# Token tiles split by ScalarE and GpSimd and transposed by DMA, an earlier key split, and four score blocks ahead of the products of differences

## The chip, the cores and the metric

The kernel runs on one core of one Trainium2 chip. A core has five engines that run their own instruction queues and meet at semaphores: TensorE (PE, matrix products into PSUM), VectorE (DVE), ScalarE (ACT), GpSimd (POOL) and SyncE (SP, which here only starts DMAs). The profile gives PE's weight loads a row of their own, PEld. The metric is the device time of one execution in microseconds; lower is better.

## The reference

The input is x, 2048 tokens of 512 numbers. With xn the layer norm of x without gain or bias, the result is the sum of three terms:

```
x + Re( DFT_seq( DFT_hid( xn ) ) ) + PEER( xn )
```

The second term is `y = Cr@(xn@Wr.T) - Ci@(xn@Wi.T)`, with cosine and sine matrices along the 2048 tokens and along the 512 numbers. The third is a mixture of 4096 tiny experts: 32 heads make a query of 2 x 128 numbers each, each half is scored against 64 keys (`s1 = q1 . k1`, `s2 = q2 . k2`), the best two of each half give four pairs, the best two pairs by their sum are weighted by a softmax, and the head adds `g * gelu(xn . u[e]) * v[e]` for both experts e.

## The kernel before

There are two long stages after a short opening, and the change lies in the opening.

**Opening (0 to about 71 us).** The tokens are held as four groups g of four 128-token tiles, in a host order in which tokens that are mirror images under the DFT stand in the same partition. The groups are taken in the order `G = (1, 0, 2, 3)`. For each group `ln` makes the layer norm in place (statistics on DVE and ACT, the scaling on ACT), and `fold(k, g)` adds (k = 0) or subtracts (k = 1) mirror tokens and mirror columns on DVE, which leaves a quarter of the products to do. `main(k, g)` on PE then multiplies the folded tokens `Q[k][g]` with the matrix part `A[k, g]` in float32 and accumulates over the four groups in four PSUM banks `PP[k]`; `evict(k)` copies them out with ACT. So the sums (k = 0) take 16 such products, and the products of differences (k = 1) 16 more. They use the same four banks (pool tag `pa`), so the second set waits for `evict(0)`. `sides` makes the rows and columns that the folding leaves over, on DVE and at its end with two instructions of GpSimd (lines 440 and 441). `fold_row` and `spread` do the same for one single row on GpSimd.

Beside that the first key matrix is made. The 32 heads are worked on in 8 chunks j of four. For a chunk, query weights and keys are multiplied once (`m_mul`) to a 512x512 matrix, so that a score block is one product of tokens with it. The matrix is scaled by a power of two (`m_scale`: largest magnitude by ACT, reduced over partitions by GpSimd on line 118, then small DVE steps) and split in a high and a low half-precision part (`m_parts`: lines 219 and 220). `k16` is the split key for the later chunks.

The tokens need the same split, and transposed. `xpose(i)` does it for tile i with four PE transposes into a PSUM bank (line 475) and an ACT copy that makes the high part (line 478). The low part comes, for the eight tiles of the first two groups, from a PE product with a negative identity and another ACT copy (lines 480 and 482), and for the eight of the last two from DVE (line 484). The result `xt[i]` takes the place of the raw tile.

**Scores (about 64 to 430 us).** `scores(j, i)` for 8 chunks times 16 tiles: 12 products (four column blocks times high-high, high-low and low-high) of 128x512 into one `pa` bank, ACT copies to `ss` (line 784), DVE finds the best eight of each group of 64 (line 787) and their places (line 791). Between the blocks the next chunk's key is made: loads of its weights (`m_load`, line 134), their split (`m_prep`, lines 158 to 166, for tile parts 0 and 2 on GpSimd), the products (line 144). The memory of these buffers overlays that of the opening (pool `da`), so they can be filled only once `sides` is done. Each finished token tile is also stored to DRAM (line 845).

**Experts (430 us to the end).** Products with all of u and v, gated by a matrix made from the chosen places.

**Order.** A framework (Tile) puts the instructions of each engine in one fixed order before the run. It goes through them by program order, passes over those that by its own estimates aren't ready, and takes the next one that is. On the chip every engine and every queue then runs its list strictly in that order. SP has eight semaphores for its DMAs, so each DMA there waits for the one eight before it.

The lines below are the functions that the change touches.

Of the kernel before, what the change touches and what calls it, by code (L numbers as in the profile page):

```python
# [8 lines left out]
F32 = mybir.dt.float32  # L9
# [26 lines left out]
def tile_fnet_peer(ctx, tc, x, ca, cb, c5, wt, wf, wr, wq, kt, ut, vn, out):  # L36
# [94 lines left out]
    def m_load(j, pool, ts):  # L131
        for t in ts:
            MS[j, t] = pool(f"wq{j}_{t}")
            nc.sync.dma_start(MS[j, t], wq[j, t // 2, t % 2])
# [105 lines left out]

    MP[0] = stS.enter_context(tc.tile_pool(name="mp0", bufs=1, side="left"))
# [40 lines left out]
    FT = {}  # L282

    def ln(g, n):
# [34 lines left out]
        nc.vector.scalar_tensor_tensor(sm[:, 2], sm[:, 0], -0.5, sm[:, 1], op0=ALU.mult, op1=ALU.mult)  # L319
        nc.vector.scalar_tensor_tensor(rstd[:, g], sm[:, 2], 1.5, sm[:, 1], op0=ALU.add, op1=ALU.mult)  # L320
# [64 lines left out]
    def spread():  # L385

        for a in range(2):
            nc.gpsimd.tensor_scalar(s5p[:, a].rearrange("o t p -> o (t p)"), s5[:, 0:256], c52[:, a:a + 1], None, op0=ALU.mult)
# [61 lines left out]
    def turn(dst, src, b=None):  # L450
# [3 lines left out]
        if b is None:  # L454
            nc.scalar.activation(d, v, AF.Copy)
            return
        for a in range(2):
            nc.scalar.activation(d[..., a::2], v[..., a::2], AF.Identity, bias=b[:, a:a + 1])
# [7 lines left out]
    idn = cst.tile([P, P], F16, name="idn")  # L466
    nc.gpsimd.tensor_scalar(idn, ident, -1.0 / XS, None, op0=ALU.mult)

    def xpose(i, sub=False):

        p = (pb if sub and i % 2 else pc)(f"xp{i}")
        src = xn(i // 4, i % 4)
        for kd in range(KD):
            c = slice(kd * P, (kd + 1) * P)
            nc.tensor.matmul(p[:, c], src[:, c], ident, start=kd == 0, stop=kd == KD - 1 and not sub,  # L475
                             is_transpose=True, skip_group_check=True)
        pv = p.rearrange("p (k n) -> p k n", k=KD)
        nc.scalar.activation(xt[i][:, 0], pv, AF.Copy, scale=XS)
        if sub:
            nc.tensor.matmul(p, idn, xt[i][:, 0].rearrange("p k n -> p (k n)"), start=False, stop=True,  # L480
                             skip_group_check=True)
            nc.scalar.activation(xt[i][:, 1], pv, AF.Copy, scale=XS)
            return
# [949 lines left out]
```

## Time and profile before

| | us |
|---|---|
| median of 3 runs (lowest, highest) | 1161.41 (1159.83, 1162.46) |
| time of the profiled execution | 1159.45 |
| its span, first to last instruction | 1157.7 |
| PE busy in the span | 1136.5 |
| DVE busy | 934.5 |
| ACT busy | 610.6 |
| GpSimd busy | 245.0 |
| PE from 0 to 34.37 | 20.39 busy |
| PE from 34.37 to 63.60 | 28.85 busy |
| PE from 63.60 to 71.11 | 7.51 busy |

The profiled execution took 1.75 us more than its span, and 1.96 us less than the median of the runs. Times in rows are counted from the span's start. A row of the timeline gives the start, the duration, the engine, the line of the kernel, the operation, what it writes and reads, how many were merged into the row, and in brackets how long the engine had been idle before and what ended that. `PE p L403` are the float32 products of `main`; each of the 32 products shows as two records. `xp` is the bank of a transposed tile, `s` a score block, `m` the key matrix, `ft`, `ff`, `fo` and `q` are the steps of a fold, `pw` the key's power of two, `zt` the transposed routing codes of the third stage. A queue row such as `SPq` is the time in which the queue was held by starting a DMA, not the transfer.

### The profile page before, as it was taken

To read this page: it belongs to the slowest core of one execution; us is meant where nothing else is said; L and a number is where in the kernel's file an instruction comes from. 1 tells how busy PE (TensorE), PEld (TensorE's weight loads), DVE (VectorE), ACT (ScalarE), POOL (GpSimd) and SP (SyncE) were. 2 spreads that over 40 slices of the span, in tenths; PEclk is the share of its full clock that TensorE was granted. 3 is DMA by queue.
4 is the path that set the end of the run, shared out by engine and by line. 5 is a ranking of instruction groups with operands and counts; after the bars stand their busy time and mean duration, and the time that the engine had idled before them with its cause. 6 is when DMAs were issued, how large, how long until landed. Compare 5 with 4: busy or idle time off the path is not lost.

```text
span 1157.7 us, 25371 instructions
## 1 busy us (share of the span) xinstructions
PE 1136.5 (98%) x9930; PEld 724.9 (63%) x9930; DVE 934.5 (81%) x2840; ACT 610.6 (53%) x1056; POOL 245.0 (21%) x232
## 2 busy tenths in 40 slices
PE   6899999999999999999999999999999999999997
PEld 4355555445445459778478479569569559658763
DVE  7987989798898999974994895897886786788670
ACT  5575687687776635354435435535535435433440
POOL 5232464865865410000000000010010000000000
PEclk9999999999999999999999999999999999999999
DMA  9182344243241204261743743644554555451423
GB/s 364 49 294 64 124 139 169 70 164 119 83 159 52 82 11 126 87 213 37 237 157 104 229 166 107 223 159 137 186 163 169 168 174 168 155 174 56 137 75 104
DMA packets 81504, 163.64 MB, mean 141 GB/s; under 512 B 16084, under 2 KB 31323, under 8 KB 81374
## 3 DMA queue, kind: packets, MB, share of 16 engines
q1 hardware_dynamic: 81008, 161.84, 42.2%
q8 instruction: 80, 1.31, 0.5%
q14 instruction: 50, 0.41, 0.1%
q10 hardware_dynamic: 302, 0.08, 0.0%
q0 software_dynamic: 64, 0.00, 0.0%
HBM read 142.69 MB, written 17.63 MB: 138 GB/s over the span
## 4 chain that ended last, share of the span: by engine, by line
PE 93%; DVE 3%; DMA 2%; ACT 1%; issue 0%; POOL 0%; SPq 0%; ACTq 0%; POOLq 0%; DVEq 0%
PE s L779 29%; PE z L908 28%; PE v L991 27%; PE g L946 4%; PE p L403 2%; PE m L144 2%; DVE L L936 1%; PE xp L475 0%; DMA xb<-in_x_dram 0%; DMA x<-in_x_dram 0%; DMA cx<-in_wt_dram 0%; DMA fit<-v_d 0%; DVE act L962 0%; DMA y<-y_d 0%; DVE w L954 0%
## 5 line engine op out<-in xcount | busy, mean ns | idle before, releaser
L908 PE MATMUL z<-xb,u 128*128 128x256 f16 (+1 forms) x3840 | 342.9, 251 | 0.2
L991 PE MATMUL v<-v,act 128*128 128x512 f16 x1536 | 338.6, 379 | 0.0
L908 PEld LDWEIGHTS <-u 128*128 128x128 f16 x3840 | 309.8, 98 | 26.8 <-issue 0.5
L779 PE MATMUL s<-m,xq 128*128 128x512 f16 x1344 | 297.3, 379 | 0.0
L991 PEld LDWEIGHTS <-act 128*128 128x128 f16 x1536 | 147.4, 98 | 171.0
L779 PEld LDWEIGHTS <-xq 128*128 128x128 f16 x1344 | 129.6, 98 | 150.3 <-issue 0.2
L936 DVE TENSOR_TENSOR L<-io_lam,cmp 128x2048 f16<-128x2048 f16 x128 | 155.9, 1218 | 59.1 <-PE g L946 58.9
L915 ACT ACTIVATE act<-z,scl 128x256 f32<-128x256 f32 (+1 forms) x224 | 100.6, 498 | 171.5 <-PE z L908 171.4
L787 DVE MAX8 vals<-ss 128x8 f32<-128x64 f32 x1024 | 152.6, 216 | 12.6 <-ACT ss L784 12.3
L1004 POOL TENSOR_TENSOR y<-y,xr 128x512 f32<-128x512 f32 x15 | 25.2, 1679 | 611.9 <-DMA y<-y_d 455.8
L961 ACT ACTIVATE act<-w 128x1024 f16<-128x1024 f32 x52 | 69.9, 1360 | 92.8 <-DVE w L954 92.1
L791 DVE FIND_INDEX8 idx<-vals,ss 128x8 uint16<-128x256 f32 x256 | 107.2, 419 | 0.0
L954 DVE SCALAR_TENSOR_TENSOR w<-act,scl,g 128x1024 f32<-128x1024 f32 x64 | 80.9, 1274 | 29.7 <-ACT act L915 29.7
L1067 ACT ACTIVATE cx<-cx 128x896 f32<-128x896 f32 x64 | 60.5, 945 | 72.3 <-DVE cx L1047 53.7
L784 ACT ACTIVATE ss<-s,wsc 128x512 f32<-128x512 f32 x112 | 74.7, 680 | 44.3 <-PE s L779 36.6
L962 DVE TENSOR_TENSOR act<-w,act 128x1024 f16<-128x1024 f32 x64 | 84.9, 1328 | 4.2 <-ACT act L961 4.2
L1041 DVE TENSOR_TENSOR cx<-cx 128x512 f32<-128x512 f32 (+2 forms) x84 | 48.4, 610 | 28.0 <-DMA cx<-in_cb_dram 25.0
L946 PEld LDWEIGHTS <-L 128*128 128x128 f16 x2048 | 60.6, 96 | 11.2 <-DVE R L944 1.2
L946 PE MATMUL g<-R,L 128*128 128x32 f16 x2048 | 61.7, 176 | 0.2 <-DVE R L944 0.2
L944 DVE TENSOR_TENSOR R<-R,cmp 128x512 f16<-128x512 f16 x128 | 59.2, 463 | 1.5
L166 POOL TENSOR_TENSOR wq<-wq,wh 128x1024 f16<-128x1024 f32 x26 | 55.4, 2133 | 12.1 <-DVE xq L484 7.9
L941 DVE TENSOR_TENSOR R<-io_c,cmp 128x512 f16<-128x512 f16 x128 | 54.5, 426 | 0.0
(290 smaller groups left out, 1094.3 us busy)
## 6 DMA issues: line engine op xcount, KB each, us to landing
v<-v_d SPq DMA_DIRECT2D x67, 512.0 KB, 4.2
cx<-in_cb_dram SPq DMA_DIRECT2D x64, 448.0 KB, 4.7
wq<-in_wq_dram SPq DMA_DIRECT2D x32, 512.0 KB, 6.0
fit<-in_wq_dram SPq DMA_DIRECT2D x28, 512.0 KB, 5.3
uv<-in_vn_dram SPq DMA_DIRECT2D x16, 512.0 KB, 3.8
uv<-in_ut_dram SPq DMA_DIRECT2D x16, 512.0 KB, 6.4
c<-in_ca_dram SPq DMA_DIRECT2D x8, 512.0 KB, 10.7
y<-y_d SPq DMA_DIRECT2D x16, 256.0 KB, 2.7
```

Of the source, the lines that this page charges most:

```text
L779: nc.tensor.matmul(ps, xt[i][:, l, kd, :], m[:, r, kd, :], start=(n == 0), stop=(n == 3 * KD - 1))
L784: nc.scalar.activation(s.rearrange("p g e -> p (g e)"), ps, AF.Copy, scale=inv)
L787: nc.vector.max(vals[:, i, w, :, h], s[:, g, :])
L791: nc.vector.max_index(idx[:, i, w].rearrange("p k h -> p (k h)"), vals[:, i, w, 0:2].rearrange("p k h -> p (k h)"), s[:, w * HC:g + 1, :]. ...
L908: nc.tensor.matmul(ps if n == 1 else ps.rearrange("p (b n) -> p b n", b=2), ug[:, l, c % 2, kd, :], xb2[:, k0, r, kd, :] if n == 1 else xb ...
L915: nc.scalar.activation(ACT[bb][:, cg * m:cg * m + m, :], pv[:, i], AF.Gelu_apprx_tanh, scale=zsc)
L936: nc.vector.tensor_tensor(L.rearrange("p t (l two) -> p t l two", two=2), io_lam.rearrange("p (l two) -> p l two", two=2).unsqueeze(1).to_ ...
L946: nc.tensor.matmul(p[:, hf, t * NC:(t + 1) * NC], L[:, t, :], R[:, t, :], start=True, stop=True)
L954: nc.vector.scalar_tensor_tensor(w, act[:, :, ts], fw, p.rearrange("p h (n c) -> p c (h n)", c=NC), op0=ALU.mult, op1=ALU.mult)
L961: nc.scalar.activation(w16[..., 0], w, AF.Copy)
L962: nc.vector.tensor_tensor(w16[..., 1], w, w16[..., 0], op=ALU.subtract)
L991: nc.tensor.matmul(pv, w16[:, c, :, l], v_sb[g][:, r, cc, :], start=(n + cc == 0 and k == 0), stop=(n == 15 and cc == 1 and k == 2))
```

## The change

- `xpose` goes, with its identity. In its place `stage(i)` lets ACT write the half-precision high part of the normalised tile and GpSimd subtract it from the tile for the low part, both in token order, into the space of the not yet loaded expert matrix `u`. One DMA transpose from SP then writes the whole `xt[i]`, both parts.
- The layer norm itself scales by 512, which the split did before; everything made from the tokens by `main` is scaled back in the copies out of PSUM (an added scale factor in instructions that were there) and, for the single row, in `spread`.
- The first group's four tiles are staged right after its sums fold. Its raw tiles get buffers of their own, since the differences are still to be made from them. The loads of the third and fourth group's difference matrices and of `wf`, `w2` and one row now stand in SP's program after these four transposes.
- `m_scale`, `m_parts` and `k16` move up from after all sums to after the third group's.
- The score blocks (chunk 0) of the first group's tiles, `s_mm`, are written in the program ahead of the products of differences, into the two `pb` and two `pc` banks. The other groups' tiles are staged in the loop of the differences, the score blocks follow the order of the groups in chunk 0.
- `zs` holds two zeros that are computed from late values, so that the `stage` copies of the first group wait for the second group's layer norm and the others for the key's scale.
- The weights of chunk 1 are loaded from GpSimd's DMA queue instead of SP's.

```diff
     def m_load(j, pool, ts):
         for t in ts:
             MS[j, t] = pool(f"wq{j}_{t}")
-            nc.sync.dma_start(MS[j, t], wq[j, t // 2, t % 2])
+            (nc.gpsimd if j == 1 else nc.sync).dma_start(MS[j, t], wq[j, t // 2, t % 2])
...
+    def s_mm(ps, m, i):
+        n = 0
+        for kd in range(KD):
+            for l, r in ((0, 0), (0, 1), (1, 0)):
+                nc.tensor.matmul(ps, xt[i][:, l, kd, :], m[:, r, kd, :], start=(n == 0),
+                                 stop=(n == 3 * KD - 1))
+                n += 1
+
+    EARLY = {}
...
+    for h in (2, 3):
+        xp[h] = da.tile([P, 2, 512], F32, name=f"x{h}")
...
+    TO = [4 * g + q for g in G for q in range(4)]
...
+    zs = da.tile([P, 2], F32, name="zs")
...
-        nc.vector.scalar_tensor_tensor(sm[:, 2], sm[:, 0], -0.5, sm[:, 1], op0=ALU.mult, op1=ALU.mult)
-        nc.vector.scalar_tensor_tensor(rstd[:, g], sm[:, 2], 1.5, sm[:, 1], op0=ALU.add, op1=ALU.mult)
+        nc.vector.scalar_tensor_tensor(sm[:, 2], sm[:, 0], -0.5 * XS, sm[:, 1], op0=ALU.mult, op1=ALU.mult)
+        nc.vector.scalar_tensor_tensor(rstd[:, g], sm[:, 2], 1.5 * XS, sm[:, 1], op0=ALU.add, op1=ALU.mult)
...
-            nc.scalar.activation(d, v, AF.Copy)
+            nc.scalar.activation(d, v, AF.Copy, scale=1.0 / XS)
...
-    def xpose(i, sub=False):
-
-        p = (pb if sub and i % 2 else pc)(f"xp{i}")
+    def stage(i):
+
         src = xn(i // 4, i % 4)
-        for kd in range(KD):
-            c = slice(kd * P, (kd + 1) * P)
-            nc.tensor.matmul(p[:, c], src[:, c], ident, start=kd == 0, stop=kd == KD - 1 and not sub,
-                             is_transpose=True, skip_group_check=True)
-        pv = p.rearrange("p (k n) -> p k n", k=KD)
-        nc.scalar.activation(xt[i][:, 0], pv, AF.Copy, scale=XS)
-        if sub:
-            nc.tensor.matmul(p, idn, xt[i][:, 0].rearrange("p k n -> p (k n)"), start=False, stop=True,
-                             skip_group_check=True)
-            nc.scalar.activation(xt[i][:, 1], pv, AF.Copy, scale=XS)
-            return
-        nc.vector.scalar_tensor_tensor(xt[i][:, 1], pv, XS, xt[i][:, 0], op0=ALU.mult, op1=ALU.subtract)
+        n = TO.index(i)
+        t = u_sb[3 + n % 10 // 2][:, n % 2].rearrange("p a k n -> p a (k n)")
+        nc.scalar.activation(t[:, 0], src, AF.Identity, bias=zs[:, int(n > 3):int(n > 3) + 1])
+        nc.gpsimd.tensor_tensor(t[:, 1], src, t[:, 0], op=ALU.subtract)
+        nc.sync.dma_start_transpose(xt[i].rearrange("p a k n -> p (a k) n"), t.rearrange("p a d -> p (a d)"))
...
-    for g in G:
+    for g in G[:2]:
         load(1, g)
     wfs = uf[14][:, 0:512]
-    nc.sync.dma_start(wfs, wf)
-    nc.sync.dma_start(w2, wr[:, 0:2].to_broadcast([P, 2]))
-    row512(1, A[1, 0][0:1, 512:1024])
...
         fold(0, g)
+        if n == 1:
+            nc.scalar.activation(zs[:, 0:1], rstd[:, g, 0:1], AF.Copy, scale=0.0)
+            for q in range(4):
+                stage(4 * G[0] + q)
+            for h in G[2:]:
+                load(1, h)
+            nc.sync.dma_start(wfs, wf)
+            nc.sync.dma_start(w2, wr[:, 0:2].to_broadcast([P, 2]))
+            row512(1, A[1, 0][0:1, 512:1024])
...
+        if n == 2:
+            m_scale(0, MS[0, "p"], FF[0, g][:, 0, 0:1])
+            m_parts(0, MS[0, "p"])
+            nc.scalar.activation(zs[:, 1:2], wsc[:, 0:1], AF.Copy, scale=0.0)
+            nc.scalar.activation(k16[:, 0], k_sb, AF.Copy, scale=sk)
+            nc.vector.scalar_tensor_tensor(k16[:, 1], k_sb, sk, k16[:, 0], op0=ALU.mult, op1=ALU.subtract)
     evict(0)
-    m_scale(0, MS[0, "p"], FF[0, G[-1]][:, 0, 0:1])
-    m_parts(0, MS[0, "p"])
-    nc.scalar.activation(k16[:, 0], k_sb, AF.Copy, scale=sk)
-    nc.vector.scalar_tensor_tensor(k16[:, 1], k_sb, sk, k16[:, 0], op0=ALU.mult, op1=ALU.subtract)
+    for i in TO[0:4]:
+        EARLY[0, i] = (pb if i % 2 else pc)(f"s0_{i}")
+        s_mm(EARLY[0, i], M[0][0], i)
     for n, g in enumerate(G):
         fold(1, g)
...
         main(1, g)
         if n:
             for q in range(4):
-                xpose(4 * G[n - 1] + q, n < 3)
+                stage(4 * g + q)
     sides()
     evict(1)
-    for q in range(4):
-        xpose(4 * G[-1] + q)
...
-        def scores(j, i, vals, idx):
+        def scores(j, n, vals, idx):
             m, inv = M[j]
...
+            i = n if j or safe else TO[n]
+            ps = EARLY.pop((j, i), None)
+            if ps is None:
+                ps = pa(f"s{j}_{i}")
+                s_mm(ps, m, i)
```

More of the change, by code (lines that the diff above doesn't have):

```diff
@@ L568, in sums @@
             nc.tensor.matmul(b8[:, 2 * n:2 * n + 2], a256[:, g // 2, c:c + P], w2, start=True, stop=True)
-        nc.scalar.activation(p256, b8[:, 0:16].rearrange("p (n a) -> p n a", n=8), AF.Copy)
+        nc.scalar.activation(p256, b8[:, 0:16].rearrange("p (n a) -> p n a", n=8), AF.Copy, scale=1.0 / XS)
         b5 = pc("b5")
@@ L771, in compact @@
             CMP[b] = cmp
-        def scores(j, i, vals, idx):
+        def scores(j, n, vals, idx):
             m, inv = M[j]
-            ps = pa(f"s{j}_{i}")
-            n = 0
-            for kd in range(KD):
-                for l, r in ((0, 0), (0, 1), (1, 0)):
-                    nc.tensor.matmul(ps, xt[i][:, l, kd, :], m[:, r, kd, :], start=(n == 0),
-                                     stop=(n == 3 * KD - 1))
-                    n += 1
+            i = n if j or safe else TO[n]
[3 more added lines that the diff above has]
+                s_mm(ps, m, i)
             st = sp.tile([P, 520], F32, tag="s", name=f"ss{j}_{i}", bufs=3 if safe else 4)
```

13 lines of the change are left out of this document (6 added, 7 removed).

## The prediction

> **What bounds the kernel now.** I read the page's totals first, then the chain that ended last.
>
> ```profile
> span 1157.7 us, 25371 instructions
> PE 1136.5 (98%) x9930; PEld 724.9 (63%) x9930; DVE 934.5 (81%) x2840; ACT 610.6 (53%) x1056; POOL 245.0 (21%) x232
> PE 93%; DVE 3%; DMA 2%; ACT 1%; issue 0%; POOL 0%; SPq 0%; ACTq 0%; POOLq 0%; DVEq 0%
> ```
>
> PE is busy for 98% of the span and holds 93% of the chain. What leaves PE's list, or lets it go on sooner, moves all that follows; elsewhere only a new wait of PE counts. The change lies in the opening, so next comes the chain there, cut to the stretch from the third group's sums to the last PE transpose, with two pieces further on, and PE's clock by stretches.
>
> ```profile
> by line: PE p L403 62.6%; PE xp L475 15.5%; PE s L779 9.4%; PE xp L480 5.6%; ACT xq L482 3.2%; ACT xq L478 1.4%; ACT xb L478 1.4%; issue 1.0%
> ...
> 62.05 1.72 PE p L403 x4
> ...
> 80.61 0.70 PE m L144 x24
> 81.31 2.59 PE s L779 x12
> ```
>
> ```profile
> 35.21:38.62 3.41, 3.41 (x5) 1.35 (x4) 3.34 (x6) 0.21 (x1) 0.99 (x2) 0.50 0.06 1
> 30.21:34.37 4.16, 0.00 (x1) 0.00 (x0) 3.74 (x10) 2.43 (x5) 4.02 (x7) 1.00 0.35 130
> ```
>
> The first line covers 34.37 to 71.11, 36.74 us. The reader is to see that token transposing holds PE's path for 15.5 + 5.6 + 3.2 + 1.4 + 1.4 = 27.1%, 10.0 us. A record of `main` takes 1.72 / 4 = 0.43 us, a score block 2.59, a quarter of a key matrix 0.70. After 4.16 us without work PE was granted half its clock for 3.41 us, which costs 1.7.
>
> For comparison I need one point that both kernels pass: four score blocks and all of `main` done. By 71.11 PE had 9.4% of 36.74 = 3.5 us of score work behind it; four blocks are 10.4, so the kernel before reaches the point at 71.11 + 6.9 = 78.0.
>
> **The change, part by part.** PE loses the 10.0 us; the four early blocks and `main` only change places. PE's floor is then the end of the sums plus 10.4 us of blocks plus 32 x 0.43 = 13.8 us of differences. What makes it later are the key, the tiles and the next key. Their rows:
>
> ```profile
> 32.13 2.93 ACT L333 ACTIVATE xq<-xq,negm,rstd 128x512 f32<-128x512 f32 x4 [1.73 <-DVE negm L321]
> 41.46 0.68 ACT L196 ACTIVATE m<-m,fo 128x512 f16<-128x512 f32 x1
> 47.97 0.18 ACT L201 ACTIVATION_READ_ACCUMULATOR m<-k_sb 128x1 f32 x1
> ```
>
> ```profile
> 21.72 1.23 DVE L351 TENSOR_TENSOR fo<-ft 128x2 f32<-128x2 f32 x1
> 34.23 0.42 DVE L373 TENSOR_TENSOR q<-fo 128x257 f32<-128x257 f32 x1
> 36.95 0.15 DVE L351 TENSOR_TENSOR fo<-ft 128x2 f32<-128x2 f32 x1
> 38.95 0.42 DVE L372 TENSOR_TENSOR q<-fo 128x257 f32<-128x257 f32 x1
> 49.47 0.17 DVE L119 TENSOR_SCALAR pw<-pw 128x3 f32<-128x3 f32 x1 [0.29 <-POOL pw L118]
> 51.45 2.72 DVE L220 SCALAR_TENSOR_TENSOR m<-m,msc,m 128x512 f16<-128x512 f32 x4
> 61.45 2.46 DVE L410 SCALAR_TENSOR_TENSOR u<-q,c5s,u 128x257 f32<-128x257 f32 x6
> ```
>
> ```profile
> 11.09 0.24 POOL L77 IOTA iof<- 128x128 f32 x1 [10.16 <-issue]
> 21.68 1.25 POOL L378 TENSOR_TENSOR r<-x 1x512 f32<-1x512 f32 x1
> 35.33 0.87 POOL L390 DMA_DIRECT2D s5c<-s_d  x1
> 48.29 1.15 POOL L118 PARTITION_ALL_REDUCE pw<-mx  x1 [12.09 <-ACT m L201]
> 60.37 4.67 POOL L440 TENSOR_TENSOR u<-u,r 1x512 f32<-1x512 f32 x1 [10.93 <-DVE u L431]
> 65.01 0.72 POOL L441 TENSOR_TENSOR u<-u,r 1x257 f32<-1x257 f32 x1
> 73.67 2.13 POOL L166 TENSOR_TENSOR wq<-wq,wh 128x1024 f16<-128x1024 f32 x1 [7.94 <-DVE xq L484]
> ```
>
> ```profile
> L77 POOLq MODIFY_POOL_CONFIG  x2: 11/11/11, 0.9 to 1.0; - x2
> ...
> L118 POOLq MODIFY_POOL_CONFIG  x4: 4/20/37, 36.5 to 81.1; - x4
> ...
> L440 POOLq MODIFY_POOL_CONFIG  x2: 82/82/83, 49.4 to 49.4; - x2
> ```
>
> *Subtractions of the first group.* The nearest row is L166, the same types at double width: 2.13 / 2 = 1.07 us. Four are 4.3, in GpSimd's list between 21.6 and 26, where DVE's norms and folds are what PE waits for. GpSimd and DVE get in each other's way there: the two-column add L351 took 1.23 us while L378 ran and 0.15 later. So the sums end later by 0 (GpSimd was busy with other such adds before) to 4.3 us (DVE stands through all four). I take 1.2, nearer the low end. The last sums fold was ready at 39.4 and then took 8 records, 3.4 us: 42.8, now 44.0.
>
> *Floor.* 44.0 + 10.4 + 13.8 = 68.2.
>
> *The key.* It may start after the third fold (34.65) and ACT's last norm (35.06). ACT's part took from 41.46 to 48.15 with evictions in between, 6.7 us, so it is done by 41.8 at the latest. Then GpSimd reduces. But L118 is preceded by a pair of MODIFY_POOL_CONFIG, by its name a switch of GpSimd's code library; it went off at 36.5, when GpSimd had done its earlier work. Another such pair is needed before ordinary work goes on, and one stands at the kernel's start, ahead of the 10.16 us before L77 that waited on nothing the profile shows. Around L118 both lay in GpSimd's waits of 12.09 and 10.93 us. Now GpSimd is free only after its old work (36.2) plus 4.3, plus 1.0 that I allow for being held up by DVE: 41.5. With 0 to 10.2 us of switch, and 1.15 of reduction, it ends between 43.0 and 52.8. From its end (49.44) to the first low part (51.45 + 0.68) it was 2.7: the key serves PE from 45.7 to 55.5. I take the far end, since 10.16 is the one switch that lies open. By then PE can have done the differences of two groups, 16 records or 6.9 us (44.0 to 50.9), or of three (54.3), as the planner has it. PE waits 0 to 4.6, and 1.7 more for the half clock if it waits the full length; I take 2.5. The point moves to 70.7.
>
> On the switch the Trainium skill (GPSIMD Engine Reference, section Instruction dispatch) says that the first call to a freshly loaded kernel pays about 6 us. The trace's open case is 10.16 us, and I go by it; by the page, the key would come some 4 us sooner, the 2.5 us wait would go, and the sum below would be 2.5 us better.
>
> *The other tiles.*
>
> ```profile
> L768 SPq DMA_TRANSPOSE zt<-z x2: 1183/1248/1312, 431.8 to 433.8; - x2
> ```
>
> ```profile
> c<-in_ca_dram SPq DMA_DIRECT2D x8, 512.0 KB, 10.7
> zt<-z_d SPq DMA_TRANSPOSE x14, 3.7
> ```
>
> A transpose of three 128x128 blocks held SP's queue for 1.2 us and landed 3.7 after its issue. The new ones have eight blocks. Held time: 1.2 if it goes by the DMA, 8/3 of it, 3.3, if it goes by size; I take 2.1, and 2.5 more until it has landed. GpSimd may subtract once its library is back, up to 10.2 us after 52.8: 63.0, first subtraction 64.1, first tile 68.7. PE asks for it at 70.7, so 2.0 us of cover are left. If DVE keeps GpSimd out to the end of `sides` (63.9 before, 65.1 now), the first tile comes at 70.8. At 3.3 a transpose plus a store in between, twelve tiles run slower than the blocks and cost up to 5. I take 1.0: the point is at 71.7.
>
> The four transposes of the first group hold SP for 4 x 1.2 to 3.3 from about 23 on, and the last two difference matrices queue behind them. Issued by 36 and with the median landing of 10.7, they are there at 47, and PE asks for them after 50.9: nothing.
>
> *The next key.*
>
> ```profile
> 65.76 1.76 SPq L134 DMA_DIRECT2D wq<-in_wq_dram  x4
> ```
>
> ```profile
> 70.38 1.15 ACT L158 ACTIVATE wh<-wq,ss 128x1024 f16<-128x1024 f32 x1
> ```
>
> Its four loads went out when L441 had ended (65.73), and its weights were split on GpSimd by 73.67 + 2.13 = 75.8, 10.1 us later; PE took them at 80.61. Now L440 and L441 can come after twelve more subtractions, 63.0 + 12.8 = 75.8, plus 2 to 5.4 of their own, and the loads follow them in GpSimd's queue: ready 10.1 later, at 88 to 91. PE gets to the old place of the first quarter, behind the fifth block, at 74.3. It has other blocks to do if the planner's list puts them first (two banks of four-deep buffers, 20 us). So 0 to 17 us; I take 1.5, near the low end, because the planner passes over what isn't ready.
>
> *At no cost.* ACT:
>
> ```profile
> L478 ACT ACTIVATE xq<-xp 128x512 f16<-128x512 f32 x14 | 7.9, 597 | 1.9 <-PE xp L475 1.8
> L297 ACT ACTIVATE q<-xb 128x512 bf16<-128x512 f32 x2 | 1.3, 632 | 1.2 <-DMA xb<-in_x_dram 1.2
> L484 DVE SCALAR_TENSOR_TENSOR xq<-xp,xq 128x512 f16<-128x512 f32 x8 | 5.2, 686 | 2.5 <-ACT xq L478 2.5
> ```
>
> 16 copies of about 0.63 replace 24 of about 0.6, 10 against 14 us; DVE loses 5.2. The scale by 512 adds no instruction. Scores of the early blocks can be copied out only when `sides` has left its memory, which PE's eight banks cover for 20 us.
>
> **Sum.** The point was at 78.0 and is at 71.7; less 1.5 for the next key the gain is 4.8 us. The profiled execution's 1159.45 becomes 1154.7; against the median, which lies 1.96 higher, 1161.41 - 4.8 = 1156.6.
>
> **Rivals.**
> (a) *GpSimd becomes the bound (slower).* L440, one row of 512, took 4.67 us from 60.37 while DVE's sums of `sides` ran without a gap to 63.9. If each of the twelve subtractions costs that, the last tile is ready at 63.0 + 56 + 4.6 = 123.6. PE wants it at 70.7 + 11 x 2.59 + 4 x 0.70 = 102.0. It waits 21.6, and the gain without tile wait (5.8) turns to a loss of 15.8: 1177.2. It decides from 3.4 us a subtraction (63.0 + 12 x 3.4 + 4.6 = 108.4, 6 late). Against it: L166 took 1.07 per 512 among score instructions, which follow `sides`. If only the first six are slow, the sixth comes at 95.6 where PE wants it at 70.7 + 5 x 2.59 + 3 x 0.70 = 85.8, and the time is 1165.4.
> (b) *The next key is late (slower).* If the planner keeps the old place, PE stands from 74.3 to 88: 13.7 us, 1161.41 - 6.3 + 13.7 = 1168.8. It decides from 6.3 us. For it: the loads moved behind busy GpSimd; against: the list is made anew.
> (c) *The waits eat the gain (no change).* Key wait 4.6 + 1.7 and tile wait 2 instead of 2.5 and 1.0 take the gain to 0: 1161.4.
> (d) *No waits.* Switch as fast as needed, tiles in time: 78.0 - 68.2 = 9.8, with no delay of the sums 11: 1151.
> (e) *Transposes go block by block.* If a transpose of eight takes 8/3 x 3.7 = 9.9 us and the next waits for it, the last of twelve lands at 64.1 + 119 = 183 where PE wants 102: 81 us late, about 1237. Against it: the second of the two from SBUF was started 2.0 us after the first. The Trainium skill (VectorE: DVE Perf Modes, The three transpose paths) has 390 ns on TensorE against 1309 ns by DMA for one 128x128 and advises TensorE where PSUM will do; eight blocks at that price are an estimated 10.5 us, the same case. The held time of 1.2 us for three blocks speaks against it.
>
> **How the numbers follow.** Forecast (gain 2.3 to 8): 0.43. (d), gain over 8: 0.15. (c): 0.14. (a): 0.12. (b): 0.12. (e): 0.04. A measurement of this kernel tells about 0.2%, 2.3 us, from no change. Faster 0.43 + 0.15 = 0.58, same 0.14, slower 0.28. The likeliest case alone runs from 1153.4 to 1159.1. The range goes from (d) less its last tenth, 1150.5, to (b), 1169, which leaves out (e) and the worse half of (a).
>
> **What the changed profile would show.** No `xp` rows on PE, sixteen transposes on SP with a held time of about 2.1 us, GpSimd subtractions of 1.07 us in the open and longer beside DVE. The point (four blocks and 32 products done) at about 72. L118 at 50 to 53 with an idle time put to issue, then a gap before the next GpSimd row of up to 10 us. I am wrong if PE stands over 6 us in one place before 100 us, if the subtractions take over 3.4 us, or if the first key quarter comes later than 90 with PE idle before it.

## The result, and the profile after

The changed kernel is slower. Its median is 1174.09 us over 4 runs (1171.8 to 1175.55) against 1161.62 over 4 runs of the kernel before beside them: ratio 1.0108, 95% interval 1.0086 to 1.0129. The forecast was 1156.6 with a range of 1150.5 to 1169, so sign and range both missed; the slowdown of 1.1% is small, but clear of the noise. The profiled execution took 1175.55, its span is 1173.8 (before 1159.45 and 1157.7): 16.1 us more.

Where these 16.1 us arise shows in one long window. Its columns are the stretch, its length, busy time and instructions of PE, PE's weight loads, DVE, ACT and GpSimd, then PE's granted clock, DMA share and GB/s. Before, then after:

```profile
0.00:133.00 133.00, 118.64 (x644) 67.00 (x645) 111.49 (x420) 84.33 (x177) 52.37 (x63) 0.99 0.49 175
```

```profile
0.00:133.00 133.00, 101.25 (x478) 54.46 (x479) 111.62 (x355) 69.87 (x151) 68.89 (x65) 0.90 0.63 200
```

PE stood idle for 133 - 118.64 = 14.4 us before and 31.7 after, 17.3 more. In half-microsecond windows, busy time times (1 - clock) adds up to 1.7 us lost to a lower clock before and 9.4 after, 7.7 more. That is 25.0 us lost. After 133 us PE has no long gap in either kernel (8.2 us of idle time in all after the change, 6.9 before), which makes it 26.3. The span grew by 16.1, so the work that PE was relieved of is worth about 10 us; its transposes held 7.8 of that (21.1% of 36.74) on the chain before. The change delivered its saving and lost about two and a half times as much, some 70% of it in waits and the rest in a lower clock.

The third group's sums on PE before the change:

```profile
34.37 15.90 PE L403 MATMUL p<-c,q 128*128 128x512 f32 x32 [4.16 <-DVE q L372]
```

PE's timeline after the change, up to the first product of the next key:

```profile
26.44 5.40 PE L419 MATMUL p<-c,q 128*128 128x512 f32 x8 [1.21 <-DVE q L387]
39.53 5.87 PE L419 MATMUL p<-c,q 128*128 128x512 f32 x8 [7.69 <-DVE q L387]
47.13 3.70 PE L419 MATMUL p<-c,q 128*128 128x512 f32 x8 [1.74 <-DVE q L387]
50.67 10.52 PE L245 MATMUL s<-m,xq 128*128 128x512 f16 x48
61.03 13.90 PE L419 MATMUL p<-c,q 128*128 128x512 f32 x32
74.76 4.91 PE L245 MATMUL s<-m,xb 128*128 128x512 f16 x22
91.02 0.59 PE L144 MATMUL m<-sums,wh 128*128 128x64 f16 x8 [11.35 <-ACT ss L639]
```

Here line 419 is `main` (403 before), 245 a score block, 144 a product of the next key. PE waits 7.69 us for the third group's fold, whose products start at 39.53 (34.37 before). The sums end at 50.8. Then four blocks and 32 products run without a gap to 74.8, the point that the kernel before reaches at 78.0: there the change is still 3.2 us ahead. After 22 more score products PE stands for 11.35 us, because the next key's weights aren't there.

Why they aren't is read on GpSimd, ACT and DVE. GpSimd (488 is the subtraction, 456 and 457 the end of `sides`, 134 the loads):

```profile
44.95 0.39 POOL L118 PARTITION_ALL_REDUCE pw<-mx  x1 [5.76 <-DVE fo L373]
53.03 6.00 POOL L488 TENSOR_TENSOR u<-xb,u 128x512 f16<-128x512 f32 x2 [7.69 <-ACT u L471]
59.00 18.24 POOL L488 TENSOR_TENSOR u<-xq,u 128x512 f16<-128x512 f32 x10
77.99 1.43 POOL L456 TENSOR_TENSOR u<-u,r 1x512 f32<-1x512 f32 x1 [0.76 <-DVE u L447]
82.30 0.90 POOL L457 TENSOR_TENSOR u<-u,r 1x257 f32<-1x257 f32 x1 [2.87 <-DVE u L426]
83.49 2.33 POOL L134 DMA_DIRECT2D wq<-in_wq_dram  x4 [0.30 <-POOL u L457]
```

```profile
83.23 1.26 ACT L795 ACTIVATE ss<-s,msc 128x512 f32<-128x512 f32 x2 [7.67 <-POOL u L457]
89.77 1.15 ACT L158 ACTIVATE wh<-wq,ss 128x1024 f16<-128x1024 f32 x1 [2.96 <-DMA wq<-in_wq_dram]
```

DVE, in the third and the last fold of the sums and in `sides`:

```profile
27.25 2.43 DVE L384 TENSOR_TENSOR ft<-xq,xq 128x1024 f32<-128x1024 f32 x1
32.03 3.04 DVE L333 SCALAR_TENSOR_TENSOR ff<-mvs,ff 128x4 f32<-128x4 f32 x1
42.91 0.16 DVE L203 TENSOR_REDUCE mx<-mx 128x1 f32<-128x4 f32 x1 [0.98 <-ACT m L196]
44.04 0.43 DVE L372 TENSOR_TENSOR fo<-ff 128x256 f32<-128x256 f32 x1 [0.98 <-ACT ff L371]
45.37 0.17 DVE L119 TENSOR_SCALAR pw<-pw 128x3 f32<-128x3 f32 x1 [0.57 <-POOL pw L118]
67.30 2.66 DVE L424 TENSOR_SCALAR u<-c,ft 128x512 f32<-128x512 f32 x2
69.89 6.33 DVE L426 SCALAR_TENSOR_TENSOR u<-c,q,u 128x512 f32<-128x512 f32 x4
76.14 3.57 DVE L447 SCALAR_TENSOR_TENSOR u<-c,q,u 128x256 f32<-128x256 f32 x4
```

`sides` ended at 83.20 (65.73 before) and only then gave up its memory: the copies of the scores (795) and the loads (134) start within 0.3 us of it. The first load was used at 89.77. A subtraction took 1.82 us in the row of ten and 3.0 in the row of two. The twelve took 24.2 us, 2.0 each, not the 3.4 each at which rival (a) begins, though two single ones were longer than that (shortest, median and longest in ns):

```profile
L488 POOL TENSOR_TENSOR u<-xb,u x2: 2496/3016/3536, 53.0 to 55.5; 128x512 f16<-128x512 f32 x2
L488 POOL TENSOR_TENSOR u<-xq,u x10: 1329/1599/4143, 59.0 to 75.6; 128x512 f16<-128x512 f32 x10
```

DVE's instructions grew beside them. Line 426 took 1.58 us each, 447 0.89; an instruction on four numbers per partition (333) took 3.04 (0.47 before). DVE ended its part of `sides` at 82.6, 5.4 us after the last subtraction, so it is DVE's delay that dates the end of `sides`.

### The profile page after: what moved, and what is told of

Same layout as the page of the kernel before. It is cut to its first block, busy times and chain, and to the rows that moved or that the text cites. A ratio compares the mean times of both kernels' runs of the same rounds, so it can differ in the third digit from the quotient of the medians.

```text
span 1173.8 us, 25268 instructions
## 1 busy us (share of the span) xinstructions
PE 1133.8 (97%) x9858; PEld 719.8 (61%) x9858; DVE 948.0 (81%) x2832; ACT 607.9 (52%) x1050; POOL 272.6 (23%) x251
## 4 chain that ended last, share of the span: by engine, by line
PE 84%; DVE 9%; DMA 3%; issue 1%; ACT 1%; POOL 1%; SPq 0%; DVEq 0%; ACTq 0%; POOLq 0%
PE s L245 27%; PE z L919 26%; PE v L1002 25%; PE g L957 4%; PE m L144 2%; DVE L L947 1%; DMA cx<-in_cb_dram 1%; DVE ft L384 1%; DVE act L973 1%; DMA wq<-in_wq_dram 1%; DVE w L965 1%; DVE fo L366 0%; DMA x<-in_x_dram 0%; DVE ff L363 0%; DVE R L952 0%
## 5 line engine op out<-in xcount | busy, mean ns | idle before, releaser
L245 PE MATMUL s<-m,xq 128*128 128x512 f16 x1344 | 301.6, 383 | 0.0
L947 DVE TENSOR_TENSOR L<-io_lam,cmp 128x2048 f16<-128x2048 f16 x128 | 158.4, 1237 | 59.1 <-PE g L957 59.1
```

The source lines that it names most:

```text
L245: nc.tensor.matmul(ps, xt[i][:, l, kd, :], m[:, r, kd, :], start=(n == 0), stop=(n == 3 * KD - 1))
L947: nc.vector.tensor_tensor(L.rearrange("p t (l two) -> p t l two", two=2), io_lam.rearrange("p (l two) -> p l two", two=2).unsqueeze(1).to_ ...
```

## The experiments

Theory at the outset: GpSimd's subtractions and DVE's instructions with two inputs hold each other up, the sums and `sides` end late, and the loads that need the memory of `sides` come late. The rivals: the loads were moved to the wrong queue; PE's list has the next key too early; the memory is held by something else in any case; the key's steps, now in the middle of a fold, delay the sums. The diffs are against the changed kernel; where a run is described as another one with something added, it holds that one's edits too. The kernel before had medians of 1161.49 to 1161.95 beside them. Most times came out slower than the theories expected (`mul_late` by 6.6 us, `tail_apart` by 5.7, `tail_first` by 5.6 beyond their ranges), `key_mid` faster by 1.6; `both` and `last_none` alone lie inside. So it is mainly the traces that carry the argument.

**Is it the subtractions?** `lo_copy` leaves the low part of the tokens out: ACT writes the high part twice.

```diff
-        nc.scalar.activation(t[:, 0], src, AF.Identity, bias=...)
-        nc.gpsimd.tensor_tensor(t[:, 1], src, t[:, 0], op=ALU.subtract)
+        nc.scalar.activation(t, src.unsqueeze(1).to_broadcast([P, 2, D]), AF.Identity, bias=...)
```

> ACT writes both halves of a staged tile in one copy of 128x1024, and the subtraction on GpSimd is gone: the low part of the tokens is wrong here. Theory 1 (GpSimd's subtractions and DVE's two-input instructions hold each other up, in the sums and in sides, and with sides the memory of the next weights comes free late): the third group's sums start at 34 to 35 instead of 39.5, sides ends at 65 to 69 instead of 83.2, PE's stand of 11.35 us before the next key's first quarter is under 2 us, and the time is 1174.1 - 5 - 11 - 3 (half clock) = 1155. Rival (the weights are late because they were moved to GpSimd's DMA queue and land beside the token stores, whatever the subtractions do): sums as in theory 1, but the stand stays above 6 us and the time is 1165 to 1168.

Its 2381.5 us (ratio 2.0513, 2.0466 to 2.056) say nothing of the change: without low parts the kernel goes into a second pass (`safe` in the kernel), in which PE is busy for 1136 us once more. Only the opening is read. The third sums start at 35.87 (39.53), `sides` ends at 69.3 (83.2). But the loads still start only at 74.16:

```profile
68.55 0.72 POOL L457 TENSOR_TENSOR u<-u,r 1x257 f32<-1x257 f32 x1
74.16 2.32 POOL L134 DMA_DIRECT2D wq<-in_wq_dram  x4 [4.90 <-ACT u L471]
```

The second cause stands in the brackets: line 471 copies out the products of differences, whose operands share the memory. With four blocks put ahead of them, the products end at 73.5 and the copies at about 74. PE still waits 3.5 us for the key.

`sub_dve` lets DVE subtract all sixteen tiles, `sub_dve12` only the last twelve.

```diff
-        nc.gpsimd.tensor_tensor(t[:, 1], src, t[:, 0], op=ALU.subtract)
+        nc.vector.tensor_tensor(t[:, 1], src, t[:, 0], op=ALU.subtract)
```

> The sixteen subtractions on DVE instead of GpSimd. Theory 1: each costs DVE about 0.7 us, four ahead of the third group's sums (2.8) and twelve ahead of the end of sides (8.4), but nothing is held up any more; third group's sums at 36 to 37.5, sides ends at 73 to 76, the stand of PE shrinks to 1 to 4 us, time 1160 to 1164. Rival (it is DVE's amount of work, not the contention): no better than the changed kernel, 1172 to 1178.

> Only the twelve later subtractions on DVE; the first group's four stay on GpSimd beside the sums' folds. This parts the contention in the sums from that in sides. Theory 1a (the delay of the sums by the first four costs its full 3 to 5 us): 1170 to 1172. Theory 1b (it is hidden, because the last sums fold waits for the key's steps anyway and PE then runs at half clock): early blocks at 50.7 to 51.2 as in both kernels, time 1166 to 1168.

`sub_dve`: 1166.91 us, ratio 1.0042 (1.0028 to 1.0055), 7.2 less than the change. `sub_dve12`: 1169.32, 1.0067 (1.005 to 1.0083). So the last twelve cost 4.8 us and the first four 2.4. DVE in `sub_dve12`, the same stretch:

```profile
69.03 0.67 DVE L488 TENSOR_TENSOR u<-xq,u 128x512 f16<-128x512 f32 x1
69.81 0.88 DVE L424 TENSOR_SCALAR u<-c,ft 128x512 f32<-128x512 f32 x2
70.61 2.73 DVE L426 SCALAR_TENSOR_TENSOR u<-c,q,u 128x512 f32<-128x512 f32 x4
73.26 1.66 DVE L447 SCALAR_TENSOR_TENSOR u<-c,q,u 128x256 f32<-128x256 f32 x4
75.37 2.46 DVE L426 SCALAR_TENSOR_TENSOR u<-q,c5s,u 128x257 f32<-128x257 f32 x6
```

The openings are alike up to the early blocks (50.76 and 50.67), DVE's rows show no idle time from there to the end of `sides` in either, and DVE's part of `sides` ends at 77.8, against 82.6 after the change (80.16 + 2.46 there), though DVE makes twelve more instructions of 0.67, 8.0 us. Twelve subtractions thus cost DVE 8 us when it makes them and 12.8 when GpSimd does. The Trainium skill (SBUF — State Buffer, Who interferes with whom) says that a DVE instruction with two inputs in SBUF contends with a GpSimd instruction that reads SBUF; these rows agree, and show both sides paying: 1.58 instead of 0.68 us for one of line 426, 2.0 on average for a subtraction, of which the quickest took 1.14. Line 424, which reads one tile, was stretched too: 1.33 instead of 0.44.

The first four act in a roundabout way. Without them the third sums start at 36.07 instead of 39.49, but the early blocks start at 50.7 all the same; what remains is that DVE's list, and with it `sides`, ends 2.3 us earlier (GpSimd's last addition starts at 76.58, not 78.92).

**The queue, and PE's list.** `load_sp` puts the loads back on SP; `mul_late` has the program ask for the key's parts four blocks later.

```diff
-            (nc.gpsimd if j == 1 else nc.sync).dma_start(MS[j, t], wq[j, t // 2, t % 2])
+            nc.sync.dma_start(MS[j, t], wq[j, t // 2, t % 2])
```

```diff
-{4: 1, 5: 2, 6: 3, 7: 4, 8: 5, 9: 6}
+{8: 1, 9: 2, 10: 3, 11: 4, 12: 5, 13: 6}
```

> The weights of chunk 1 go back to SP's queue, the rest as changed. In SP's list they now stand behind all transposes and eleven token stores. Theory 1: they cannot go out before sides has ended at 83, and behind the stores about 86.5; the stand of PE is as long or 3 us longer, time 1174 to 1178. Rival (the move of the loads to GpSimd's queue made them late): they go out some time before 80 and the time is 1162 to 1168.

> The products of the next key are written four score blocks later, so that in PE's list 9 blocks stand ahead of the first quarter instead of 5.8. Theory 1 (PE stands there because the list is in that order while other blocks are ready): PE does the 3.2 blocks, 8.3 us, in the stand; what is left is 3 to 6 us, time 1165 to 1169. Rival (the blocks couldn't go on either, since the copies of the scores wait for the same memory): the stand moves behind two more blocks and the time is 1172 to 1175.

`load_sp`: 1173.71, 1.011 (1.0089 to 1.0131), with PE's wait for the key at 12.49 us: the queue is not the cause. `mul_late`: 1175.63, 1.0122 (1.0105 to 1.0139). PE's single wait of 11.35 fell apart into 1.59, 1.34 and 3.12, 6.1 us, but a new one took the gain:

```profile
94.50 0.23 PE L144 MATMUL m<-sums,wq 128*128 128x64 f16 x1 [3.12 <-POOL wq L166]
114.07 3.57 PE L581 MATMUL b<-w,u 128*128 128x2 f32 x16 [5.50 <-DVE m L220]
```

By the bracket, the later key still held the banks that the small products `b` need. That a list which asks later would be faster remains open; this edit wasn't.

**The key in the middle of the fold.** `key_mid` is `sub_dve` with the key's steps (`m_scale`, `m_parts`, `k16`) written after the fold of the last group instead of before it; `key_pool` is that alone, with the subtractions on GpSimd.

```diff
+        if n == 3:
+            m_scale(0, MS[0, "p"], FF[0, G[2]][:, 0, 0:1])
+            m_parts(0, MS[0, "p"])
...
-        if n == 2:
-            m_scale(0, MS[0, "p"], FF[0, g][:, 0, 0:1])
-            m_parts(0, MS[0, "p"])
```

> As sub_dve (subtractions on DVE), and the key's scale and split are written after the last sums fold instead of after the third. Theory 2 (beside the contention, the key's steps that were moved up stand in DVE's and ACT's lists inside the last sums fold, which there waits for ACT and for GpSimd's reduction, some 3.2 us of DVE's time): the last sums products start at 41 to 42.5 instead of 44.89, the four early blocks at 47 to 48.5 instead of 50.7, sides ends 2 to 3 us sooner, time 1163 to 1165. Rival (the last fold was late for another reason, or PE only stands longer at the next key): the last products still start after 44, or they start sooner and the stand before the next key grows by as much, time 1166 to 1168.

> The changed kernel with only the key's steps put after the last sums fold; all sixteen subtractions stay on GpSimd. Theory (PE's path after the opening is set by the end of sides, which is late through the subtractions): the last sums and the early blocks come 1 to 3 us sooner and the stand before the next key grows by the same, because sides still ends at 82 to 84; time 1172 to 1175. Rival (what the key's place costs is lost in any case): time 1168 to 1170, as 5.5 us were gained where the subtractions were on DVE.

`key_mid`: 1161.41, 1.0001 (0.9989 to 1.0012). PE's timeline:

```profile
36.09 3.70 PE L419 MATMUL p<-c,q 128*128 128x512 f32 x8 [2.06 <-DVE q L387]
41.35 3.70 PE L419 MATMUL p<-c,q 128*128 128x512 f32 x8 [1.56 <-DVE q L387]
47.47 10.52 PE L245 MATMUL s<-m,xq 128*128 128x512 f16 x48 [0.50 <-DVE m L220]
83.09 0.58 PE L144 MATMUL m<-sums,wh 128*128 128x64 f16 x8 [5.76 <-issue]
```

In `sub_dve`, with which it is compared, DVE waited for ACT and for GpSimd's reduction inside the last fold:

```profile
39.65 0.16 DVE L203 TENSOR_REDUCE mx<-mx 128x1 f32<-128x4 f32 x1 [0.63 <-ACT m L196]
40.79 0.43 DVE L372 TENSOR_TENSOR fo<-ff 128x256 f32<-128x256 f32 x1 [0.98 <-ACT ff L371]
43.14 0.17 DVE L119 TENSOR_SCALAR pw<-pw 128x3 f32<-128x3 f32 x1 [1.58 <-POOL pw L118]
```

The last sums start at 41.35 instead of 44.89, and the key is ready almost in time for the blocks at 47.47 (PE waits 0.50 for it). So these 0.63 + 0.98 + 1.58 us (0.98 + 0.98 + 0.57 after the change), and the key's small steps there, were a cause: 5.5 us of the total. Most of it shows in the clock: up to 133 us, PE's idle time fell only from 25.9 to 24.9 us, but the loss by the clock from 8.6 to 5.4, as the wait ahead of the last sums went from 5.12 to 1.56. `key_pool`: 1171.07, 1.0071 (1.0054 to 1.0087), a gain of only 3.0. There the third sums still start late, at 39.34, the early blocks come at 49.27, 1.4 us sooner than after the change, and the loads go out at 81.14, 2.35 sooner; PE still waits 11.50 for the key. What makes up the difference between 3.0 and 5.5 stays open.

**Are the early blocks worth their place?** `no_early` is `key_mid` without the four blocks ahead of the differences.

```diff
-    for i in TO[0:4]:
-        EARLY[0, i] = (pb if i % 2 else pc)(f"s0_{i}")
-        s_mm(EARLY[0, i], M[0][0], i)
```

> As key_mid, without the four score blocks ahead of the products of differences. It prices that part of the change. Theory (the blocks fill the time in which PE would wait for DVE's folds of the differences): PE has gaps of 6 to 8 us between 45 and 67, fewer blocks are done when it stands at the next key, whose weights come no sooner; time 1164 to 1167. Rival (the blocks only change places, and differences done sooner release the memory sooner): release before 73, time 1158 to 1161.

1168.21, 1.005 (1.0033 to 1.0067), 6.8 us worse than `key_mid`: PE then waits 1.34 and 2.95 us around DVE's folds of the differences and 1.21 for ACT's copy of the sums. The blocks do fill these.

**The memory.** `wq_apart` (on `sub_dve`) and `both` (on `key_mid`) load three of the four weight tiles into memory that `sides` doesn't hold, from SP ahead of the differences; the staged tiles then share six places instead of ten. `sides_first` is `key_mid` with the last eight tiles staged behind `sides()`. `sides_apart` is `both` and `sides_first` together, its loads held back by an ACT write that waits for the key's scale.

```diff
+    for t, k in enumerate((12, 6, 7)):
+        MS[1, t] = uf[k].rearrange("p (h d) -> p h d", h=2)
+        nc.scalar.activation(MS[1, t][:, 0, 0:1], wsc[:, 0:1], AF.Copy, scale=0.0)  # sides_apart only
+        nc.sync.dma_start(MS[1, t], wq[1, t // 2, t % 2])
...
```

> As sub_dve, and three of the four weight tiles of the next key are loaded into memory that the opening does not use (places of the expert matrix; the staging goes round in six places instead of ten), from SP's queue ahead of the products of differences. Theory 1 in its second half (the stand before the next key is the way from the release of the opening's memory through the load of the weights): the load, 6.5 us from issue to use, leaves the way; the first quarter comes at 81.5 to 83 instead of 85.4, the small waits after it go, and with a stand under 3.4 us perhaps the half clock too; time 1160 to 1163. Rival (the load is not what ends the stand): first quarter at 85, time 1166 to 1168.

> key_mid and wq_apart together. If the two costs stand one behind the other on PE's path, the gains add: 1166.9 - 3 - 5 = 1159, 1157 to 1161, about the kernel before or under it. Rival (both act on one wait, the release of the opening's memory by sides, so that only the larger one counts): 1161 to 1163.

> As key_mid, and the staging of the last eight tiles is written behind sides instead of ahead of it, so that DVE ends sides before the last five subtractions. Theory (the release of the opening's memory at the end of sides is what dates the next key's weights, and so PE's stand): sides ends at 71 to 73 instead of 75.3, the first quarter comes as much sooner, the stand falls from 5.76 to 2 to 3.5 us, perhaps with no half clock after it; the last eight tiles are still in time; time 1156 to 1159. Rival (the late tiles become the wait in its place): PE waits for a transposed tile between 80 and 95, time 1161 or more.

> As sides_first, and the three weight tiles in memory apart as in wq_apart, but their loads are held back until the key's scale is known. Theory: in wq_apart the loads at 34 to 36 made GpSimd's library switch longer (its reduction at 45.1 and 44.9 in the two kernels with them, 42.7 and 43.1 in the two without), so here the reduction is back at 42.7 to 43.3; with the weights there and the release at 71 to 73 PE stands under 1.5 us; time 1152 to 1156, under the kernel before. Rival (the reduction was late by chance, or the weights' split on ACT behind the score copies is the next wait): reduction at 45, or a stand of 2 to 4 us; time 1156 to 1160.

| | us | ratio (95%) | early blocks | PE's wait for the key |
|---|---|---|---|---|
| `wq_apart` | 1163.96 | 1.0019 (1.0009 to 1.0029) | 53.30 | 1.81 |
| `both` | 1160.3 | 0.9991 (0.9981 to 1.0001) | 49.22 | 1.17 |
| `sides_first` | 1164.56 | 1.002 (1.0008 to 1.0033) | 47.31 | 6.84 |
| `sides_apart` | 1159.77 | 0.9986 (0.9974 to 0.9997) | 46.97 | 4.06 |

Loads of its own memory cut the wait from 5.66 to 1.81, yet `wq_apart` gained only 3.0 us on `sub_dve`, because its early blocks came 2.6 later: while the loads ran, GpSimd's reduction for the key came 8.63 us after its last work, not 6.47. Holding the loads back (`sides_apart`) brought 6.47 again:

```profile
42.71 0.39 POOL L118 PARTITION_ALL_REDUCE pw<-mx  x1 [6.47 <-issue]
```

```profile
45.12 0.39 POOL L118 PARTITION_ALL_REDUCE pw<-mx  x1 [8.63 <-issue]
```

```profile
42.59 0.39 POOL L118 PARTITION_ALL_REDUCE pw<-mx  x1 [6.47 <-DVE ff L368]
```

These are `sub_dve`, `wq_apart` and `sides_apart`. In `sides_first` DVE ended its part at 70.3, but GpSimd's one-row addition, started earlier, took 7.67 us beside it, and the end of `sides` stayed where it was:

```profile
66.77 7.67 POOL L456 TENSOR_TENSOR u<-u,r 1x512 f32<-1x512 f32 x1 [23.44 <-DVE u L447]
```

**The end of `sides`.** `tail_first` and `tail_apart` are `sides_first` and `sides_apart` with that addition and its neighbour on DVE, and one dummy number added on GpSimd early. `last_none` is `tail_apart` with the tiles staged ahead of `sides` again and one later load (line 657) on ACT's queue; `last_four` is the same with four tiles behind `sides`.

```diff
-        nc.gpsimd.tensor_tensor(a256[0:1, 0], a256[0:1, 0], r[:, 0], op=ALU.add)
-        nc.gpsimd.tensor_tensor(a5[0:1, 0], a5[0:1, 0], r[:, 1, 0:257], op=ALU.add)
+        nc.gpsimd.tensor_tensor(r[:, 1, 400:401], wsc[0:1, 0:1], wsc[0:1, 0:1], op=ALU.add)
+        nc.vector.tensor_tensor(a256[0:1, 0], a256[0:1, 0], r[:, 0], op=ALU.add)
+        nc.vector.tensor_tensor(a5[0:1, 0], a5[0:1, 0], r[:, 1, 0:257], op=ALU.add)
```

> As sides_first, and the two one-row additions that end sides are made by DVE instead of GpSimd (a one-element addition stays on GpSimd so that its library is switched back early). Theory (GpSimd was kept from its addition by DVE, and this addition alone dated the release of the memory): release at 71 to 72 instead of 75.2, first quarter of the next key at 77.5 to 79 instead of 82.1, stand of PE 2.5 to 4 us, time 1158 to 1161. Rival (the memory waits for the products of differences or their copies too): release after 74, time 1163 to 1165.

> The same on sides_apart. Theory: release at 71 to 72 instead of 74.8, first quarter at 74 to 75 instead of 77.9, stand under 1.5 us, time 1154 to 1157, under the kernel before with its interval. Rival (the next wait takes the place: the low parts of the weights on GpSimd, or the copies of the scores): 1158 to 1160.

> As tail_apart, but the late tiles are staged ahead of sides again, as in key_mid, and the second load for the expert matrix's largest value goes out from ScalarE's queue instead of SP's. Theory (the transposes collided with loads once they came behind the release): all transposes are issued by 71 at about 1.35 us each, release at 74 to 75, first quarter of the next key after 6 blocks at 77 to 78.5 with a stand under 2.5 us, no wait of PE over 1 us between 90 and 110; time 1154 to 1157.5. Rival (something else of the staging costs it): 1159 or more.

> The same with the last four tiles behind sides. Theory: two to three transposes still fall behind the release and beside loads and are held 2 us or more each; release at 72.5 to 74, stand under 2 us, small waits after it; time 1155 to 1159, not better than last_none. Rival (an earlier release is worth more than the collision): better than last_none by 1 us or more.

`tail_first`: 1166.56, 1.0042 (1.0029 to 1.0056). `sides` let go at 71.27, as wanted, and the loads went out at 71.89, but ACT got the first only at 82.87. SP's queue and ACT's timeline:

```profile
71.80 18.91 SPq L490 DMA_TRANSPOSE xq<-u  x5
```

```profile
82.87 1.15 ACT L158 ACTIVATE wh<-wq,ss 128x1024 f16<-128x1024 f32 x1 [8.90 <-DMA wq<-in_wq_dram]
```

Five transposes beside the loads held SP for 3.8 us each on average. After the change one held it for 1.28 us, the median in the middle of these three, and landed 3.3 us after its issue:

```profile
L489 SPq DMA_TRANSPOSE xq<-u x14: 1231/1280/1362, 30.7 to 77.6; - x14
```

`tail_apart`: 1162.71, 1.0008 (0.9998 to 1.0019). PE's wait for the key was down to 0.31, but the transposes (2.4 each) kept SP's queue, a later load came 5.50 us late to ACT, and PE paid 3.08:

```profile
98.82 1.01 PE L604 MATMUL b<-one,u 128*128 128x1 f32 x4 [3.08 <-DVE m L225]
```

`last_none` makes two changes to `tail_apart`, which no run takes apart. It starts its last transpose at 69.6, and the one load that still waits for `sides` goes out at 74.78. It is the fastest: 1157.34 (1155.19 to 1160.15), 0.9965 (0.9951 to 0.9978), 4.4 us below the kernel before and 16.8 below the change. `last_four`: 1159.42, 0.9981 (0.9968 to 0.9994). `last_none`, the window of the first views and PE:

```profile
0.00:133.00 133.00, 113.67 (x628) 61.74 (x629) 119.31 (x457) 83.52 (x176) 46.92 (x62) 0.99 0.68 212
```

```profile
47.00 10.52 PE L250 MATMUL s<-m,xq 128*128 128x512 f16 x48 [0.49 <-DVE m L225]
57.36 13.04 PE L424 MATMUL p<-c,q 128*128 128x512 f32 x30
77.22 0.34 PE L149 MATMUL m<-sums,wh 128*128 128x64 f16 x6 [1.00 <-issue]
```

Idle time is 19.3 us instead of 31.7, the wait for the key 1.00, and in the half-microsecond windows the clock costs 1.5 instead of 9.4.

## What held and what failed of the prediction

**Held.** PE's relief, and that new waits could spoil it. The sixteen transposes are free: 1.28 us held each (2.1 forecast), and PE never waited for a tile after the early blocks. PE's wait for the first key's low part, forecast 2.5 us, is none. The key was reduced 7.5 us sooner than the far end that I took (45.3 against 52.8): GpSimd's idle time ahead of it is 5.76, not 10.16. Here the Trainium skill (GPSIMD Engine Reference, Instruction dispatch: about 6 us for a first call) was the better guide, as the 5.8 to 7.5 of the runs without loads beside it show.

**Step "subtractions of the first group", sums later by 1.2.** Failed: the sums end at 50.8, not 44.0. The bound of 4.3 took GpSimd's own busy time as the most that DVE could lose, but the third sums came 5.2 late (3.5 of it undone in `sub_dve`). And the step counted no cost of the key in the last fold: DVE's fixed order has the key's steps in its middle. `key_mid` shows 5.5 us. I had asked when the key may start, and not what queues behind it.

**Step "next key", 1.5 of 0 to 17.** The step that decided the sign. The chain was right in that the loads came behind `sides`, its rows gave 88 to 91, and the first quarter came at 91.0. That it fell into this range is partly luck: the subtractions began at 53.0, not 63.0, but took 24.2 us, not 12.8; `sides` ended with DVE's part and not with them; and the first product came 7.8 us after that end, ahead of GpSimd's split of the weights, up to which my 10.1 us count. What failed is the choice near the low end, "because the planner passes over what isn't ready": PE's list has the quarter after 5.8 blocks, and the chip waits there, 11.35 us. With the half clock after it (busy 3.98 us of 84.9 to 95, so 2.0 lost) it cost more than its length. This is rival (b), for which I had a chance of 0.12 and 1168.8; it came with the late sums on top. Two of my three signs of being wrong came in full (PE stood over 6 us in two places, 7.69 and 11.35, and the quarter came later than 90 with PE idle), the third in two single subtractions of over 3.4 us.

**Rival (a)** looked at the wrong engine. Two subtractions took 3.5 and 4.1 us, but the twelve only 2.0 on average, and PE waited for none. DVE was the one whose delay counted, and through it `sides`, the memory and the loads; `sub_dve` gets 7.2 us back though GpSimd was never late with a tile.

**What the list of rivals lacked** is that the four blocks themselves hold back the memory: in `lo_copy` `sides` ends at 69.3, and the loads still wait until 74.16 for the copies of the differences. Sooner blocks ease it (with the key's steps moved, in `tail_first`, the loads go out at 71.89); memory apart takes three of the four loads off this wait.

**The sum.** The point of four blocks and 32 products came at 74.8 (71.7 forecast, 78.0 before): the sums were 6.8 us later than forecast, and the 3.5 us that I had put down for waits after them didn't come. Then the key cost what it cost. Of the 16.8 us between the change and `last_none`, 7.2 are the subtractions' engine, 5.5 the key's place in the fold, and 4.1 memory, loads and the end of `sides`. These shares hold for the edits made in this order: with the subtractions left on GpSimd, the key's place was worth 3.0. That `last_none` lies 4.4 below the kernel before, about the 4.8 that I had forecast for the change, is no confirmation, since it holds further edits.

## To carry to other kernels

When work goes to an idle engine, ask which busy engine slows down beside it: here twelve subtractions took more of DVE's time when GpSimd made them (12.8 us) than when DVE did (8.0). When something is put ahead in an engine's fixed order, follow the memory that the pushed-back work gives up, and what loads into it. And a wait worked out as "0 to 17" goes to the end that the in-order list makes likely, not to the end that a clever planner would.

## What the runs showed of the hardware that I had not expected

PE's clock was halved without an idle gap that the profile shows. After the change, the first of these windows holds 26 products of one or two columns (`b`, lines 581 to 591) and the end of a score block, and in the second PE counts as busy throughout:

```profile
109.90:113.10 3.20, 3.20 (x27) 3.15 (x26) 3.17 (x21) 0.87 (x2) 0.00 (x0) 0.86 0.01 3
112.40:119.00 6.60, 6.60 (x20) 2.75 (x21) 1.52 (x12) 0.78 (x3) 0.00 (x0) 0.50 0.00 1
```

That is 3.3 us lost. Such a dip of 3.3 or 6.6 us follows these products in 13 of the 18 traces (in `mul_late`, `tail_apart`, `tail_first` and `last_four` with an idle gap of 5.50, 3.08, 1.27 and 0.89 us among or just ahead of them; in `mul_late` it is longer), and not in those of the kernel before, `lo_copy`, `wq_apart`, `both` and `last_none`. What decides it stays open. One trace is one execution, and it may differ between executions of one kernel: of the ten of `last_none`, four have a mean clock of 0.997, the traced one among them, and take 1155.19 to 1157.49 us, six have 0.994 or 0.995 and take 1156.8 to 1160.15. So the dip may be a part of what separates the medians of neighbouring kernels.

GpSimd's reduction for the key followed its last work by 5.8 to 7.5 us without loads, and by 8.6 to 8.8 beside 1.5 MB of them (`wq_apart`, `both`). A DMA transpose of eight blocks held its queue 1.3 us, and beside loads up to 6.9 (`tail_first`, landed after 12.1). A GpSimd addition of one row of 512 took 1.43 (after the change), 4.65 (`sub_dve`) or 7.67 us (`sides_first`), each beside DVE's work in `sides`; in `tail_first` DVE made it in 0.67. How GpSimd and DVE share their way to memory instruction by instruction, these traces don't resolve.
